# Transform along d of pairs 3 and 4 in two parts by lo, side by side in halves of the array's columns

## The chip, the cores and the metric

The kernel runs on one core of one Trainium2 chip. The metric is the device time of one execution in microseconds (us), the median of several runs. Profiles come from one more execution that the hardware profiler watched; its own time stands beside its span in the table below. Engines are named as the profile names them: PE (TensorE, the matrix multiplier), PEld (its weight loads), DVE (VectorE), ACT (ScalarE), POOL (GpSimd), SP (SyncE, which only issues DMAs here).

## The reference

Two kinds of layer alternate, twice each, on x of shape 1 x 2048 x 448 (S positions, D channels) in bf16:

```python
def _A_ref(x, w_r, w_i):
    X = rfft2(x.astype(float32), axes=(-2, -1))
    X = X * (w_r + 1j * w_i)
    return irfft2(X, s=(S, D), axes=(-2, -1)).astype(bfloat16)

def _B_ref(x, w1, b1, w2, b2):
    h = x @ w1 + b1
    h = relu(h) ** 2
    return h @ w2 + b2

x = x + _A_ref(layernorm(x), A_w_r, A_w_i)
x = x + _B_ref(layernorm(x), B_w1, B_b1, B_w2, B_b2)   # and both once more
```

`_A_ref` is a filter in the frequency domain: a Fourier transform over both axes, a product with complex weights, and the transform back. `_B_ref` is a feed-forward block with a squared relu and F = 1792.

## The kernel before, in words

**The spectral layer as matmuls.** A position s is split as s = 128 hi + lo, with hi from 0 to 15 and lo from 0 to 127. The layer goes through these stages, whose names are also the names of code:

- A: for each of 16 tiles of positions, a transform over hi together with the layer norm (`first_A`, `second_A`). Its result goes to `XA`, with d on the partitions and 16 components c of 128 values lo each. A tile t holds the eight values lo from 8t to 8t+7, so the first half of lo (0 to 63) is complete when tiles 0 to 7 are evicted, the second half with tile 15. The components are the real and imaginary parts (e = 0 and 1) of "pairs": pair p from 1 to 7 is components 2p and 2p+1; components 0 and 1 are the two real ones.
- TD: the transform along d (`stage_TD`), with a 128-column slice of `XA` as weights and the table `TD_sb` streaming. Its result, lo on the partitions, is evicted from PSUM to `U` in SBUF (`TD_out`).
- B: the transform over lo (`stage_B`), from `U` through the tables `G_sb` and `GN_sb` into `EF`.
- W: the product with the complex weights on DVE (`stage_W`), from `EF` into `Z`: first pair 1 alone, then pairs 2 and 3, then 4 and 5, then 6 and 7, then components 0 and 1.
- Bi, TI, AI: the transforms back; AI's result is added to x on DVE (L1147).

The feed-forward layer then computes h (`h_part`, `h_pairs`) and the output tiles o (`o_tile`), PE's large part of the work. In the first feed-forward layer each output tile is followed by the second spectral layer's stage A for that tile (`second_A`), so that the second TD follows the last tiles of the first feed-forward layer. Dummy matmuls (L1416, `warm_mm`) are put in where the planner sees PE idle for long.

**Pairs 1 and 2 in halves.** `TD_half` (L912) computes one e of pairs 1 and 2 together. It has two parts h = 0 and 1, one for each half of lo, and each is a unit of its own: the weights are 64 columns of `XA`, the matmuls of pair 1 and pair 2 alternate, and they go to different halves of the array's columns, and so to different halves of the PSUM partitions (s in L920). Part 0 needs only stage A's tiles 0 to 7. For the second pair of the two the halves of lo come out exchanged, and row L106 exchanges the rows of its table `G` to match. Each of the two pairs has a PSUM bank for itself and a 448-column eviction. Pair 4 (it is in `SPLIT`) has a bank and a 448-column eviction for each e, with full 128-column weights; pair 3 has two banks and one 896-column eviction for both e.

**What sets the order.** Each matmul group, eviction or vector operation is a unit, numbered in the order in which the code makes it. The strings in `ORDER` (L115) list for each engine the units in the order in which that engine issues them; an engine runs its list strictly in that order, and semaphores make it wait for what a unit needs. PSUM has eight banks, which are given out along the list of PE. The units that matter here, by their numbers before the change:

- First layer: 156 is the last of stage A on PE, 157 and 160 evict its last tiles. TD of pairs 1 and 2: 161 and 162 (e = 0, part 0 and 1), evicted by 163 (pair 1) and 164 (pair 2); 165 and 166 (e = 1), evicted by 167 and 168. B of pair 1: 169 and 171, evicted by 170 and 172. W of pair 1: 173 to 180. B of pair 2: 181 and 183. TD of pair 3: 185. B of pair 3: 187 and 189. TD of pair 4: 199 and 201. TD of pair 5: 207.
- Second layer: 857 is stage A of the last tile on PE, evicted by 858 (pairs 0 to 3) and 859 (pairs 4 to 7). TD of pairs 1 and 2: 860 and 861, 864 and 865, evicted by 862, 863, 866, 867. B of pair 1: 868 and 870, evicted by 869 and 871; of pair 2: 880 and 878, evicted by 881 and 879. W of pair 1: 872 to 877. TD of pair 3: 882. B of pair 3: 884, evicted by 885. TD of pair 4: 894 and 896.

Of the kernel before, what the change touches and what calls it, by code (L numbers as in the profile page):

```python
# [25 lines left out]
MERGE = (1, 2, 3, 4, 5)  # L26

# [9 lines left out]
def make_constants():  # L37
# [68 lines left out]
    G[:, 3] = np.roll(G[:, 3], 64, axis=0)  # L106
# [20 lines left out]
1354""",  # L127
    "act": """
# [12 lines left out]
1310 1313 1315 1318 1320 1323 1325 1330 1328 1335 1333 1338 1340""",  # L141
    "dve": """
# [438 lines left out]
def bass_interleave_layers__spectral_gfnet__dense_activation_squared_relu__prompt_kernel(nc, A_x, A_w_r, A_w_i, B_x, B_w1, B_b1, B_w2, B_b2, out):  # L581
# [6 lines left out]
    with ExitStack() as es:  # L588
# [220 lines left out]
        q = _Tile(1)  # L809
# [102 lines left out]
        def TD_half(first, e):  # L912
# [26 lines left out]
            for i in range(2):  # L939
                TD_out(q[i], 2 * (1 + i) + e, 1, first, ("act", "dve"))  # L940
# [554 lines left out]
```

## Time and profile before

| What | Value |
|---|---|
| Time, median of 3 runs | 266.68 us (266.57 to 267.13) |
| The profiled execution | 267.61 us, its span 265.0 us |
| PE busy | 255.3 us (96%), 2127 matmuls |
| DVE busy | 203.7 us (77%) |
| ACT busy | 175.8 us (66%) |
| POOL busy | 14.2 us (5%) |
| Granted PE clock | 1.00 (mean) |

The time of the profiled execution is larger than the span by what lies before the first and after the last instruction (2.6 us). Rows of the timeline begin with the start in us from the span's start and the length; equal neighbours are put together with their count, and idle time of the engine before them stands in brackets with what ended it. A row of windows gives a stretch, its length, and the busy time of each engine in it with the number of instructions.

### The profile page before, as it was taken

How to read it: one execution, taken by the hardware profiler on the slowest of the kernel's cores; microseconds unless marked ns; L12 is line 12 of the kernel's file. 1: busy time of each engine (PE TensorE's matmuls, PEld its weight loads, DVE VectorE, ACT ScalarE, POOL GpSimd, SP SyncE). 2: the span in 40 equal slices, each digit the busy share in tenths (PEclk: the TensorE clock that was granted, in tenths of full speed). 3: DMA queues.
4: the chain of work that ended last, by engine and by line, in shares of the span. 5: the costliest groups of instructions: out<-in, count | busy, mean ns of one | idle time of the engine just before them, and what ended most of it. 6: DMA issues, size and time to landing. Idle time of an engine off the chain costs nothing. (4 is left out here: it accounts for less than half of the span.)

```text
span 265.0 us, 5678 instructions
## 1 busy us (share of the span) xinstructions
PE 255.3 (96%) x2127; PEld 160.4 (61%) x2127; DVE 203.7 (77%) x653; ACT 175.8 (66%) x380; POOL 14.2 (5%) x32
## 2 busy tenths in 40 slices
PE   6999989999999999999999998899999999999996
PEld 2786678787544554455567775788654475554454
DVE  3988998999978973779996999899974239832552
ACT  5987898987549448793326988899645886311830
POOL 8840000000000000000000000000000000000000
PEclk9999999999999999999999999999999999999999
DMA  7999700023300223000000000020341000033022
GB/s 224 388 279 342 254 0 2 0 42 71 74 2 0 43 40 66 17 0 2 0 1 2 2 0 2 0 41 5 64 92 37 5 0 2 0 89 97 18 76 82
DMA packets 25531, 16.33 MB, mean 62 GB/s; under 512 B 18174, under 2 KB 24542, under 8 KB 25504
## 3 DMA queue, kind: packets, MB, share of 16 engines
q1 hardware_dynamic: 24768, 14.25, 20.4%
q10 hardware_dynamic: 576, 0.92, 1.0%
q0 software_dynamic: 160, 0.81, 0.7%
q8 instruction: 17, 0.28, 0.4%
q14 instruction: 10, 0.08, 0.1%
HBM read 10.46 MB, written 1.84 MB: 46 GB/s over the span
## 5 line engine op out<-in xcount | busy, mean ns | idle before, releaser
L681 PE MATMUL ps<-yT,W_sb 64*128 64x512 bf16 (+1 forms) x770 | 90.4, 346 | 0.0
L681 PE MATMUL ps<-W_sb,arena 128*128 128x448 bf16 (+3 forms) x476 | 87.1, 342 | 0.0
L681 PEld LDWEIGHTS ps<-yT,W_sb 64*128 64x128 bf16 (+1 forms) x770 | 52.6, 95 | 34.2 <-ACT arena L700 1.3
L735 DVE TENSOR_TENSOR arena<-arena 128x512 bf16<-128x512 bf16 (+1 forms) x140 | 44.8, 366 | 31.0 <-ACT arena L700 30.6
L681 PEld LDWEIGHTS ps<-W_sb,arena 128*128 128x128 bf16 x476 | 45.3, 98 | 38.3 <-DVE arena L735 1.5
L700 ACT ACTIVATE arena<-ps,b1col 128x512 bf16<-128x512 f32 x84 | 52.2, 688 | 24.5 <-PE ps L681 24.4
L706 ACT ACTIVATE arena<-ps 128x448 bf16<-128x448 f32 (+1 forms) x40 | 26.0, 717 | 5.5 <-PE ps L681 5.2
L700 ACT ACTIVATE mv<-mv,epst 128x1 f32<-128x1 f32 (+1 forms) x45 | 12.8, 294 | 14.7 <-DVE mv L826 13.4
L1171 ACT ACTIVATE VT<-x_sb 128x448 bf16<-128x448 bf16 x29 | 16.8, 582 | 5.5 <-DVE x_sb L1147 5.5
L700 ACT ACTIVATE arena<-ps 128x256 bf16<-128x256 f32 x56 | 17.9, 397 | 1.4 <-PE ps L681 1.1
L717 ACT ACTIVATE arena<-x_sb,rstd 128x448 bf16<-128x448 bf16 x13 | 8.8, 673 | 14.9 <-DVE rstd L1216 10.4
L706 ACT ACTIVATE XA<-ps 128x512 bf16<-128x512 f32 (+1 forms) x27 | 14.3, 581 | 4.3 <-PE ps L681 4.3
L681 PE MATMUL ps<-H_sb,arena 128*128 128x256 bf16 x128 | 15.9, 273 | 1.3 <-DVE arena L735 0.9
L681 PE MATMUL ps<-arena,G_sb 128*128 128x448 bf16 (+1 forms) x84 | 16.4, 335 | 0.2 <-ACT arena L706 0.2
L681 PE MATMUL ps<-yT,VT 64*128 64x512 bf16 x42 | 15.8, 376 | 0.0
L706 ACT ACTIVATE VT<-ps 128x1024 bf16<-128x1024 f32 (+2 forms) x20 | 14.1, 786 | 2.2 <-PE ps L681 2.1
L735 DVE TENSOR_TENSOR tmp<-arena,Wt 128x896 bf16<-128x896 bf16 x26 | 15.4, 622 | 0.1
L1293 DVE SCALAR_TENSOR_TENSOR x_sb<-ps,mv,arena 128x448 bf16<-128x448 f32 (+2 forms) x13 | 8.3, 645 | 9.3 <-PE ps L681 9.2
L681 PEld LDWEIGHTS ps<-H_sb,arena 128*128 128x128 bf16 x128 | 11.9, 98 | 4.9 <-DVE arena L735 2.9
L681 PE MATMUL ps<-TD_sb,XA 112*128 112x112 bf16 (+3 forms) x232 | 14.3, 230 | 0.3 <-DVE arena L707 0.3
L706 ACT ACTIVATE tmp<-ps 128x896 bf16<-128x896 f32 (+1 forms) x16 | 12.9, 849 | 1.5 <-PE ps L681 1.5
L681 PEld LDWEIGHTS ps<-TD_sb,XA 112*128 112x128 bf16 (+3 forms) x232 | 12.3, 103 | 2.2 <-DVE arena L707 0.5
(84 smaller groups left out, 298.5 us busy)
## 6 DMA issues: line engine op xcount, KB each, us to landing
out_dram<-x_sb SPq DMA_DIRECT2D x15, 112.0 KB, 1.8
W_sb<-in_B_w_dram SPq DMA_DIRECT2D x1, 1568.0 KB, 12.4
W_sb<-in_B_w_dram SPq DMA_DIRECT2D x1, 1344.0 KB
xin<-in_A_x_dram ACTq DMA_DIRECT2D x4, 224.0 KB, 5.5
xin<-in_A_x_dram SPq DMA_DIRECT2D x4, 224.0 KB, 7.0
H_sb<-c_H SPq DMA_DIRECT2D x1, 896.0 KB, 7.0
G_sb<-c_G SPq DMA_DIRECT2D x1, 672.0 KB, 9.5
Wt<-in_A_w_i_dram SPq DMA_DIRECT2D x1, 393.8 KB, 5.6
```

The source lines that it names most:

```text
L681: return sch.add("pe", lambda e: e.matmul(_res(o), lhsT, rhs, start=start, stop=stop, skip_group_check=skip), [lhsT, rhs], [o], cost=cost, ...
L700: sch.add("act", lambda e: e.activation(o, _res(i), func, **kw), rd, [o], cost=c)
L706: op = sch.add(engs[0], lambda e: e.activation(o, _res(i), ACT.Copy) if h[0].eng == "act" else e.tensor_copy(o, _res(i)), [i], [o], cost=c ...
L717: op = sch.add(engs[0], lambda e: e.activation(o, i, ACT.Copy, scale=s) if h[0].eng == "act" else e.tensor_scalar(o, i, s, 1.0, op0=ALU.mu ...
L735: sch.add(eng, lambda e: e.tensor_tensor(o, _res(a), b, op), [a, b], [o], cost=_free(o) / rate + 69.0)
L1171: op = sch.add("act", lambda e, i=i, o=o, x=x, h=h: e.activation(o, x, ACT.Square, accum_out=sd[:, i, 1:2]) if h[0].eng == "act" else e.sc ...
L1293: small(lambda e: e.scalar_tensor_tensor(out=o, in0=_res(i), scalar=rs[0] if rs else 1.0, in1=xi, op0=ALU.add if t >= 4 and last else ALU. ...
```

## The change

Pairs 3 and 4 get the same treatment as pairs 1 and 2: for each e, two parts by the halves of lo, with the two pairs side by side in the halves of the array's columns. `TD_half` takes the two pairs as an argument; the rows of `G` are exchanged for pair 4, too, as they are for pair 2. Pair 3 no longer has one 896-column eviction but two of 448 columns. There are two units more in each of the two spectral layers, so that later units are renumbered, and the planner's lists of all five engines are new throughout.

```diff
+COUPLES = ((1, 2), (3, 4))
...
-    G[:, 3] = np.roll(G[:, 3], 64, axis=0)
+    for _, p in COUPLES:
+        G[:, p + 1] = np.roll(G[:, p + 1], 64, axis=0)
...
-        def TD_half(first, e):
+        def TD_half(first, e, pair):
...
-                    p, s = 1 + i, slice(64 * (h ^ i), 64 * (h ^ i) + 64)
+                    p, s = pair[i], slice(64 * (h ^ i), 64 * (h ^ i) + 64)
...
-                TD_out(q[i], 2 * (1 + i) + e, 1, first, ("act", "dve"))
+                TD_out(q[i], 2 * pair[i] + e, 1, first, ("act", "dve"))
...
-            if p == 2:
-                return
-            if p == 1:
-                for e in range(2):
-                    TD_half(first, e)
-                return
+            for pair in COUPLES:
+                if p == pair[0]:
+                    for e in range(2):
+                        TD_half(first, e, pair)
+                if p in pair:
+                    return
```

The lists of PE, the lines around the two transforms along d:

```diff
-54 70 62 104 78 107 86 94 117 120 143 146 130 133 159 156 161 165 162 166 185 171 169 207 181 187 183 189 199 201 211
-205 209 203 225 221 227 223 251 247 239 249 255 241 253 259 261 263 257 265 267 287 374 289 270 392 291 318 272 304
...
-843 822 807 837 727 860 757 857 864 861 865 882 868 870 880 878 884 902 894 896 914 904 900 898 918 938 930 920 916
...
+70 54 62 78 104 107 86 120 117 94 146 143 130 133 159 156 161 185 165 189 162 166 190 186 171 169 181 183 195 209 193
+205 213 207 227 223 211 229 225 253 241 249 251 257 243 255 265 263 259 261 267 269 289 376 272 291 394 274 293 320
...
+809 845 744 729 824 862 839 888 759 859 866 863 867 884 889 870 872 885 882 880 892 906 904 922 902 908 918 924 920
```

In the new numbers the first layer keeps 0 to 184. Pairs 3 and 4 are 185 and 186 (e = 0, part 0 and 1, evicted by 187 and 188) and 189 and 190 (e = 1, evicted by 191 and 192); B of pair 3 is 193 and 195, and units from B of pair 4 on have 2 more than before. In the second layer the units up to B of pair 2 have 2 more than before; pairs 3 and 4 are 884 and 885 (e = 0) and 888 and 889 (e = 1), evicted by 886, 887, 890 and 891; B of pair 3 is 892, and units from B of pair 4 on have 4 more.

In the new lists of the evicting engines, the first TD's evictions stand as 163, 164, 187 and then 172 on DVE, and 167, 168, 188, 170, 192, 191 on ACT (before: 163, 168, 172 on DVE and 167, 164, 170, 186 on ACT). In the second layer the old 859 goes from DVE, where it came just ahead of W of pair 1, to ACT, right behind 858; ACT then has 864, 869 (the old 862 and 867), 890, 891, 873 (the old 871), 886, 887, 883, 881, 893.

In stage A of the first layer, where x still arrives by DMA, DVE's list before has 84 (the reciprocal for tile 4, from which POOL's 85 scales the table for PE's 86) and 110 ahead of 135, the first statistics of tile 12; the new one has them behind it.

More of the change, by code (lines that the diff above doesn't have):

```diff
@@ L116 @@
     "pe": """
[10 rows of a table removed]
-1354""",
-    "act": """
[12 rows of a table removed]
-1310 1313 1315 1318 1320 1323 1325 1330 1328 1335 1333 1338 1340""",
-    "dve": """
[23 rows of a table removed]
-1339 1341 1346 1255 1343 1119 1349 1352 1355""",
[10 rows of a table added]
+1355 1358""",
+    "act": """
[12 rows of a table added]
+1117 1312 1317 1319 1314 1324 1322 1327 1329 1334 1332 1339 1337 1342 1344""",
+    "dve": """
[23 rows of a table added]
+1262 1340 1338 1343 1345 1353 1350 1347 1356 1359""",
     "pool": """
-12 15 13 16 17 14 18 20 19 22 21 53 69 61 23 77 24 85 25 116 119 26 142 145 129 132 158 155""",
+12 15 13 16 18 17 20 14 19 22 21 69 53 61 77 23 25 85 119 116 24 145 142 129 132 26 155""",
     "sp": """
-3 6 4 8 10 28 30 29 36 32 40 41 39 31 27 34 45 37 33 47 46 38 44 35 314 334 269 352 354 355 372 390 408 426 1005 1026
-1044 1046 1064 1047 1082 1100 1306 1303 1118 1297 1300 1206 1203 1250 1347 1259 1256 1212 1253 1350 1209 1344 1353
-1356""",
+3 6 4 8 10 30 28 29 38 45 36 32 35 40 34 41 31 33 46 44 27 39 47 37 316 336 354 271 356 357 374 392 410 428 1009 1030
+1048 1050 1068 1051 1086 1307 1310 1104 1301 1122 1210 1263 1216 1213 1207 1304 1260 1254 1354 1257 1351 1348 1357
+1360""",
 }
```

84 rows, old and new, of the table ORDER are left out of this document.

## The prediction

> **What bounds the kernel now.** First the page's busy times, then the windows, cut where the timeline shows the kernel's stages to change.
>
> ```profile
> PE 255.3 (96%) x2127; PEld 160.4 (61%) x2127; DVE 203.7 (77%) x653; ACT 175.8 (66%) x380; POOL 14.2 (5%) x32
> ```
> ```profile
> core 0: us, PE busy (x) PEld busy (x) DVE busy (x) ACT busy (x) POOL busy (x), PEclk, DMA share, GB/s
> 21.60:40.80 19.20, 18.28 (x139) 12.80 (x137) 18.96 (x39) 17.10 (x25) 0.00 (x0) 1.00 0.54 172
> 49.80:141.00 91.20, 91.20 (x708) 53.56 (x706) 78.54 (x303) 56.59 (x138) 0.00 (x0) 1.00 0.13 26
> 148.20:165.50 17.30, 16.13 (x163) 11.73 (x160) 17.10 (x34) 15.32 (x22) 0.00 (x0) 1.00 0.01 2
> 173.00:262.70 89.70, 89.69 (x678) 52.04 (x676) 55.47 (x158) 50.65 (x117) 0.00 (x0) 1.00 0.18 43
> ```
>
> The page alone says PE, at 96%. The windows say where that is true: in the two feed-forward layers (91.20 of 91.20 us and 89.69 of 89.70) PE has no idle time, and a start that is x us later there is passed on as x us. In the spectral layers it is DVE: 18.96 of 19.20 us and 17.10 of 17.30, from the first operation of stage W to its last, at 21.60 to 40.80 and at 148.20 to 165.50. PE idles in both. So a spectral layer ends as late as W starts, plus 19 or 17 us of DVE work that the change leaves as it is. The question is what the change does to the first W operation (pair 1's). The timelines of the three engines ahead of it, first layer (PE, DVE, ACT):
>
> ```profile
> 17.05 0.27 PE L681 MATMUL ps<-Fs,m 128*128 128x256 bf16 x1
> 17.25 1.76 PE L681 MATMUL ps<-TD_sb,XA 128*64 128x224 bf16 x32
> 19.32 0.94 PE L681 MATMUL ps<-TD_sb,XA 128*128 128x224 bf16 x8 [0.31 <-DVE arena L707]
> 20.09 0.92 PE L681 MATMUL ps<-arena,G_sb 128*128 128x448 bf16 x4
> ```
> ```profile
> 18.63 1.16 DVE L707 CAST arena<-ps 128x448 bf16<-128x448 f32 x2 [0.94 <-PE ps L681]
> 20.67 0.62 DVE L707 CAST arena<-ps 128x448 bf16<-128x448 f32 x1 [0.88 <-PE ps L681]
> 21.63 0.69 DVE L735 TENSOR_TENSOR tmp<-arena 128x448 bf16<-128x448 bf16 x2 [0.33 <-ACT arena L706]
> ...
> 24.24 0.62 DVE L735 TENSOR_TENSOR tmp<-arena,Wt 128x896 bf16<-128x896 bf16 x1
> ```
> ```profile
> 15.85 2.10 ACT L706 ACTIVATE XA<-ps 128x512 bf16<-128x512 f32 x4
> 19.02 0.98 ACT L706 ACTIVATE arena<-ps 128x448 bf16<-128x448 f32 x2 [1.06 <-PE ps L681]
> 21.05 3.68 ACT L706 ACTIVATE arena<-ps 128x448 bf16<-128x448 f32 x6 [1.06 <-PE ps L681]
> ```
>
> PE does the halves of pairs 1 and 2 (32 matmuls), waits for a bank, does pair 3 (x8), then B of pair 1 (x4, at 20.09). Its evictions end on ACT at about 21.6, and W starts at 21.63. DVE and ACT sit idle in between: the path is matmul, eviction, matmul, eviction.
>
> **The matmuls themselves cost the same.** Matmuls overlap, so I use the distance of their starts: length less one matmul, over one less than the count. The 32 halves take (1.76 - 0.26) / 31 = 0.048 us each, the 8 whole ones (0.94 - 0.26) / 7 = 0.097. Two halves for one whole: 0.39 us for a unit of 8 halves, and four units (1.56) for the three units that go (0.78 and twice 0.39). Loads double in number, of 64 columns each:
>
> ```profile
> L681 PEld LDWEIGHTS ps<-TD_sb,XA 128*128 128x128 bf16 x48 | 4.5, 98 | 1.1 <-DVE arena L707 0.5
> L681 PEld LDWEIGHTS ps<-TD_sb,XA 128*64 128x64 bf16 x32 | 1.5, 109 | 0.3 <-DVE XA L707 0.2
> L706 ACT ACTIVATE arena<-ps 128x896 bf16<-128x896 f32 x18 | 15.8, 921 | 1.4 <-PE ps L681 1.4
> L706 ACT ACTIVATE arena<-ps 128x448 bf16<-128x448 f32 x22 | 11.2, 550 | 4.1 <-PE ps L681 3.9
> ```
>
> A load of half the columns takes 109 ns instead of 98. It hides behind the other half's matmul, or the halves could not follow each other every 48 ns. (TensorEngine Tiling (Array Packing) of the Trainium skill, under Restrictions and Gotchas, says that column tiling excludes the fast weight load. The two load rows agree; with loads that were not hidden, the 32 halves would need 3.5 us and not 1.76, so the rule does not bind here.) Eviction: one of 921 and two of 550 ns become four of 550, or 620 on DVE (20.67), 0.2 to 0.3 us more in each layer, some of it on a DVE that waits anyway.
>
> **First layer: W starts 0.4 us later.** The new list of PE is 161 185 165 189, 162 166 190 186, 171 169: all first parts, then all second parts, then B of pair 1. From 17.25, eight units of 0.39 end at 20.38. Entering the split mode costs 0.20 - 0.11 = 0.09 us (17.05 to 17.25 against the normal distance of stage A); I take the same for leaving it: B can start at 20.47, where it started at 20.09. Its input is ready by then: pair 1's second part is done after six units, at 19.6; ACT starts an eviction about 0.2 after the matmuls (18.8 to 19.02) and takes 0.55, so 20.35. From B to W the path keeps its length, 21.63 - 20.09 = 1.54, since ACT's 188 is done by 21.3 and B's first result waits for ACT until 21.4: W at 22.0, **0.4 us later**. The gap that the change fills (18.8 to 19.32) lay ahead of B, but two units of second parts (0.78) came ahead of pair 1's, and two behind them; what leaves the place is one pair-3 unit of 0.78 and the wait. Bounds: 0, if B were not held up; 0.8, if pair 3's last eviction (ACT's 191, sixth in a row from 19.8, about 22.8) also holds up B of pair 3 and opens a gap in W of pairs 2 and 3. DVE gets there 24.24 - 21.63 = 2.61 after W's start, at 24.6 (24.24 is that operation's start before). Its input: B of pair 1 and the two units of pair 2 (0.19 a matmul, 0.76 a unit of four) end at 22.75, pair 3's unit waits for 191 and ends at 23.6, its eviction at 24.4. So no gap: 0.4.
>
> **Second layer: 0.1 us.** PE, DVE, ACT:
>
> ```profile
> 141.02 1.06 PE L681 MATMUL ps<-Fs,tmp 128*128 128x128 bf16 x16
> 142.01 0.58 PE L681 MATMUL ps<-TD_sb,XA 112*64 112x112 bf16 x16
> 142.82 0.40 PE L681 MATMUL ps<-Fs,tmp 128*128 128x128 bf16 x4 [0.23 <-DVE mv L744]
> 143.06 0.38 PE L1416 MATMUL ps<-ones 128*128 128x512 bf16 x1
> 143.72 0.39 PE L681 MATMUL ps<-Fs,tmp 128*128 128x64 bf16 x8 [0.29 <-DVE Fs L718]
> 144.04 0.58 PE L681 MATMUL ps<-TD_sb,XA 112*64 112x112 bf16 x16
> 144.56 0.34 PE L1416 MATMUL ps<-ones 128*128 128x256 bf16 x2
> 144.83 1.87 PE L681 MATMUL ps<-TD_sb,XA 112*64 112x112 bf16 x48
> 146.57 2.43 PE L681 MATMUL ps<-arena,G_sb 128*128 128x448 bf16 x12
> ```
> ```profile
> 145.84 1.93 DVE L707 CAST arena<-ps 128x448 bf16<-128x448 f32 x3 [2.27 <-PE ps L681]
> 147.69 0.41 DVE L707 CAST XA<-ps 128x256 bf16<-128x256 f32 x1
> 148.19 1.17 DVE L735 TENSOR_TENSOR tmp<-arena,Wt 128x896 bf16<-128x896 bf16 x2
> 149.46 0.69 DVE L735 TENSOR_TENSOR tmp<-tmp 128x448 bf16<-128x448 bf16 x2
> ```
> ```profile
> 142.63 1.91 ACT L706 ACTIVATE XA<-ps 128x512 bf16<-128x512 f32 x4
> 145.45 0.98 ACT L706 ACTIVATE arena<-ps 128x448 bf16<-128x448 f32 x2 [0.91 <-PE ps L681]
> 146.74 4.46 ACT L706 ACTIVATE arena<-ps 128x896 bf16<-128x896 f32 x7 [0.31 <-PE ps L681]
> ```
>
> Here idle PE time really lies ahead of B: PE waits for DVE's last tile (142.4 to 143.72) and then for its eviction (to 144.83). But only one first part (888) is put there; pairs 1 and 2's second parts still start at about 144.83, when ACT has evicted the tile (144.54) and two dummy matmuls are through, and B of pair 1 at 146.54, when DVE's second eviction of its input is in (146.47): before, pair 3 stood between them, now two units of halves, and both fit. ACT, behind two new evictions of 0.44 net from 146.63, reaches B's second result at 147.5; before, it had pair 3's one of 0.92 there from 146.74. W starts at 148.15. Then 885 stands ahead of B of pairs 2 and 3: 0.39 and two changes of mode at 0.09, 0.57 us. ACT then has five evictions of 0.44 from 147.5 and one of 0.92, and so the input of W of pairs 2 and 3 at 150.6 to 150.75; DVE arrives there, after two operations (148.19 to 149.46 before) and four of 0.30, at 150.6. Bounds: 0 and 0.57; I take **0.1**. The eviction at 147.69 that moves from DVE to ACT fits in ACT's idle time before 145.45. (The same page says under Tiling Modes that a change of mode drains the array: the 0.09 agrees. The new list has 18 changes for 14; by the rule all four more would cost PE 0.4 us, but two lie in its idle time.)
>
> **What else moves.** All lists are new. Where PE is at 91.20 of 91.20, another order can win nothing and may lose something. In stage A, 84 stands behind 135, which waits for x:
>
> ```profile
> 10.42 1.16 DVE L825 BATCH_NORM_STATS2 st<-xin 128x6 f32<-128x448 bf16 x2 [0.61 <-DMA xin<-in_A_x_dram]
> 12.23 0.28 PE L681 MATMUL ps<-Fs,xin 128*128 128x256 bf16 x1 [0.17 <-ACT Fs L717]
> ```
>
> PE stalls 0.33 there before (11.90 to 12.23); with tile 4's table made after 11.2 it stalls earlier instead and as long or 0.1 longer. Bounds -0.3 (the stall goes) to 0.5; I take **0.1**. The stretches between W and the feed-forward layers (40.80 to 49.80 and 165.50 to 173.00) keep their operations in nearly the same order: 0, within 0.3 either way.
>
> **The sum**: 0.4 + 0.1 + 0.1 = 0.6 us on a span of 265.0 and a profiled execution of 267.61, so 265.6 and 268.2. The median of the runs is 0.93 below the profiled execution; carried over, 266.68 + 0.6 = **267.3 us**.
>
> **The rivals.**
> - *PE is what is short* (faster). If the start of W did not count, PE's filled idle time would: 0.5 us at 18.8 and 0.39 for 888, so 0.9 less, 265.8. It decides where DVE has slack in W; 18.96 of 19.20 speaks against it. Chance 0.17.
> - *Nothing is passed on* (no change). B of pair 1 is late, but the new order makes it good in stage A or between W and h: 266.7. For it speaks the 0.33 stall in stage A. Chance 0.2.
> - *A new stall behind the halves* (slower). Eight halves hold all eight PSUM banks, and ACT has six evictions in a row; if it falls behind, B of pairs 2 and 3 opens gaps in W in both layers, 0.4 each, besides the 0.6: 268.1. It decides when the W operations of pairs 2 and 3 are reached before B's evictions; I have margins of only 0.2 and about -0.1. Chance 0.2.
> - My forecast, W later by 0.5 in all, from 266.9 to 267.8: chance 0.43.
>
> **How the numbers follow.** A measurement of this kernel can tell about 0.2%, 0.53 us, from no change. Faster has 0.17. Same: the 0.2 and a third of the forecast's 0.43 (what lies below 267.2), 0.35. Slower: the rest, 0.48. The range goes from 265.8, the first rival's own time, to 268.4, the third rival's with the 0.3 of the unknown stretches: outside lie half of the first and a quarter of the others' tails, about 2 in 10. Without the faster rival it would be 266.6 to 268.4.
>
> **What would show it.** In the changed kernel's timeline: 64 halves in one run of about 3.3 us from 17.3, B of pair 1 at about 20.5, W's first operation at 22.0 to 22.2 and then DVE without a gap over 0.2; in the second layer B to W as before relative to the last tile, and a gap of about 0.1 before W of pairs 2 and 3; PE without idle time in the feed-forward layers. The prediction is wrong if W starts at or before 21.6, if stage A ends more than 0.4 from 17.2, or if PE shows new waits in the feed-forward layers.

## The result, and the profile after

The changed kernel takes 267.16 us (median of 17 runs, 266.88 to 267.79), the kernel before 266.66 us beside it (17 runs, 266.44 to 267.29). The ratio is 1.0017, 95% interval 1.0009 to 1.0024: 0.45 us slower, with 0.24 to 0.64. The forecast was 267.3, 0.6 slower. The profiled execution of the changed kernel took 266.91 us, its span 265.1.

The busy line of its page (as before: time, share, instructions), then the windows from the first W operation to the end of the layer's DVE work and from the first to the last matmul of each feed-forward layer:

```profile
PE 257.8 (97%) x2178; PEld 166.2 (63%) x2178; DVE 203.1 (77%) x655; ACT 175.3 (66%) x381; POOL 13.6 (5%) x31
```
```profile
21.66:40.71 19.05, 18.58 (x139) 12.88 (x137) 18.88 (x38) 15.89 (x24) 0.00 (x0) 1.00 0.49 164
49.74:140.96 91.22, 91.22 (x708) 55.77 (x706) 77.61 (x302) 57.39 (x139) 0.00 (x0) 1.00 0.13 26
148.01:165.45 17.44, 15.76 (x149) 11.15 (x147) 17.20 (x34) 15.95 (x23) 0.00 (x0) 1.00 0.01 1
172.93:262.79 89.86, 89.86 (x678) 54.94 (x676) 55.88 (x161) 49.24 (x114) 0.00 (x0) 1.00 0.18 43
```

The picture is the same as before: DVE without a pause in W, PE without one in the feed-forward layers. PE's 1% more on the page is no sign of less waiting; part of it is dummy matmuls, six of them in one row (1.47 us) while PE waits for W in the first layer. The timeline around the change, PE, DVE and ACT:

```profile
16.50 0.27 PE L683 MATMUL ps<-Fs,m 128*128 128x256 bf16 x1
16.70 3.26 PE L683 MATMUL ps<-TD_sb,XA 128*64 128x224 bf16 x64
19.89 1.50 PE L683 MATMUL ps<-arena,G_sb 128*128 128x448 bf16 x7
...
36.89 1.47 PE L1418 MATMUL ps<-ones 128*128 128x512 bf16 x6
```
```profile
18.84 2.31 DVE L709 CAST arena<-ps 128x448 bf16<-128x448 f32 x4 [1.79 <-PE ps L683]
21.66 0.69 DVE L737 TENSOR_TENSOR tmp<-arena 128x448 bf16<-128x448 bf16 x2 [0.51 <-ACT arena L708]
```
```profile
19.23 1.42 ACT L708 ACTIVATE arena<-ps 128x448 bf16<-128x448 f32 x3 [1.50 <-PE ps L683]
20.86 1.42 ACT L708 ACTIVATE arena<-ps 128x448 bf16<-128x448 f32 x3 [0.21 <-PE ps L683]
```

All 64 halves run in one row of 3.26 us, and B of pair 1 starts 3.19 us after the first of them (before: 20.09 - 17.25 = 2.84). The first W operation comes 4.96 us after the first half (before 21.63 - 17.25 = 4.38). Its absolute time hardly moved, 21.66 for 21.63, because the first half itself started 0.55 earlier.

Since the start of stage A differs from run to run, I measure all kernels from the first half. In this table S is the start of the first half, B that of B of pair 1, W that of the first W operation, h that of the first matmul of the feed-forward layer; "W length" goes to the start of W's last operation; "FF2" is from the first to the last matmul of the second feed-forward layer. FF2 goes to the end of its last matmul; all others are differences of starts in the timelines. The ratio is to the kernel before, measured beside each (medians 266.60 for e1 to e4, 266.63 for e5 to e8, 266.69 for e9 to e12).

| Kernel | Time, us | Ratio, 95% interval | S to B | B to W | W length | S to h | FF2 |
|---|---|---|---|---|---|---|---|
| before | 266.66 | | 2.84 | 1.54 | 18.79 | 32.55 | 89.72 |
| after | 267.16 | 1.0017 (1.0009 to 1.0024) | 3.19 | 1.77 | 18.66 | 33.04 | 89.86 |
| e1 before, new stage A | 267.49 | 1.0038 (1.0025 to 1.0052) | 3.39 | 1.53 | 18.78 | 33.09 | 89.72 |
| e2 after, old stage A | 267.33 | 1.0030 (1.0019 to 1.0041) | 3.19 | 1.77 | 18.66 | 33.04 | 89.85 |
| e3 before, 4 matmuls ahead of B | 268.39 | 1.0069 (1.0055 to 1.0083) | 2.84 | 2.30 | 18.78 | 33.30 | 90.65 |
| e4 after, other order | 267.66 | 1.0037 (1.0025 to 1.0048) | 2.94 | 1.54 | 19.18 | 33.29 | 89.86 |
| e5 before, 7 matmuls in Bi | 268.35 | 1.0064 (1.0050 to 1.0078) | 2.84 | 1.54 | 18.78 | 33.26 | 90.65 |
| e6 before, 2 matmuls ahead of B | 268.21 | 1.0053 (1.0040 to 1.0066) | 2.85 | 1.91 | 18.77 | 32.92 | 90.64 |
| e7 after, order found later | 267.37 | 1.0022 (1.0012 to 1.0031) | 2.53 | 1.95 | 19.10 | 33.00 | 89.85 |
| e8 before, B of pair 1 earlier | 266.77 | 1.0009 (0.9998 to 1.0021) | 2.15 | 1.96 | 18.95 | 32.45 | 89.95 |
| e9 before, 4 matmuls at the start | 267.90 | 1.0042 (1.0029 to 1.0055) | 2.84 | 1.54 | 18.79 | 32.55 | 90.60 |
| e10 e8, eviction back on ACT | 266.60 | 0.9997 (0.9988 to 1.0006) | 2.15 | 1.57 | 19.26 | 32.36 | 89.72 |
| e11 e7 with three changes | 266.75 | 0.9999 (0.9990 to 1.0008) | 2.53 | 1.56 | 19.02 | 32.53 | 89.71 |
| e12 e2, one eviction to ACT | 267.66 | 1.0039 (1.0026 to 1.0052) | 3.19 | 1.54 | 19.02 | 33.17 | 89.86 |

Read the first two lines: 0.49 us in the first layer (+0.35 to B, +0.23 from B to W, -0.13 in W, the rest behind it), and 0.14 in the second feed-forward layer. Between them, from h to the first matmul of the second feed-forward layer, it is 123.17 before (172.97 - 49.80) and 123.19 after. In the second spectral layer small terms cancel: PE and DVE of the changed kernel,

```profile
141.72 0.58 PE L683 MATMUL ps<-TD_sb,XA 112*64 112x112 bf16 x16
...
144.13 2.32 PE L683 MATMUL ps<-TD_sb,XA 112*64 112x112 bf16 x80
146.39 0.93 PE L683 MATMUL ps<-arena,G_sb 128*128 128x448 bf16 x4
147.25 0.58 PE L683 MATMUL ps<-TD_sb,XA 112*64 112x112 bf16 x16
```
```profile
148.01 1.17 DVE L737 TENSOR_TENSOR tmp<-arena,Wt 128x896 bf16<-128x896 bf16 x2 [0.41 <-ACT arena L708]
149.28 0.69 DVE L737 TENSOR_TENSOR tmp<-tmp 128x448 bf16<-128x448 bf16 x2
150.08 0.69 DVE L737 TENSOR_TENSOR arena<-tmp 128x448 bf16<-128x448 bf16 x2
150.69 1.16 DVE L737 TENSOR_TENSOR tmp<-arena,Wt 128x896 bf16<-128x896 bf16 x2
```

The first half (141.72) comes 91.98 us after h, 0.23 sooner than before (142.01 - 49.80 = 92.21); B of pair 1 comes 4.67 behind it (before 146.57 - 142.01 = 4.56), and the row of DVE from the first W operation to its end is 17.44 us long (before 165.50 - 148.19 = 17.31). W of pairs 2 and 3 (150.69) follows without a wait for B. The gap of 0.1 us stands ahead of 150.08, where an operation reads what the one right before it wrote, and not where I looked for it.

### The profile page after: what moved, and what is told of

It reads as the page before. It is cut to its first block, busy times and chain, and to the rows that moved or that the text cites. A ratio compares the mean times of both kernels' runs of the same rounds, so it can differ in the third digit from the quotient of the medians.

```text
span 265.1 us, 5774 instructions
## 1 busy us (share of the span) xinstructions
PE 257.8 (97%) x2178; PEld 166.2 (63%) x2178; DVE 203.1 (77%) x655; ACT 175.3 (66%) x381; POOL 13.6 (5%) x31
## 4 chain that ended last, share of the span: by engine, by line
PE 81%; DVE 13%; issue 3%; DMA 1%; ACT 1%; DVEq 0%
PE ps L683 81%; DVE tmp L737 8%; DVE arena L737 3%; DMA xin<-in_A_x_dram 1%; ACT arena L708 1%; PE ps L1418 1%; DVE VT L709 1%; DVE x_sb L1149 0%; DVE st L827 0%; DVE VT L1174 0%; DVE VT L737 0%; DVE x_sb L1295 0%; DVE mv L828 0%; DVE x_sb L741 0%; DVEq L1431 0%
## 5 line engine op out<-in xcount | busy, mean ns | idle before, releaser
L683 PEld LDWEIGHTS ps<-yT,W_sb 64*128 64x128 bf16 (+1 forms) x770 | 56.6, 95 | 29.0 <-ACT arena L702 2.0
L708 ACT ACTIVATE arena<-ps 128x448 bf16<-128x448 f32 (+1 forms) x41 | 25.3, 698 | 5.2 <-PE ps L683 5.0
L683 PE MATMUL ps<-TD_sb,XA 112*64 112x112 bf16 (+3 forms) x280 | 14.3, 229 | 0.0
L683 PEld LDWEIGHTS ps<-TD_sb,XA 112*64 112x64 bf16 (+3 forms) x280 | 12.7, 106 | 2.2 <-issue 0.8
L683 PEld LDWEIGHTS ps<-arena,G_sb 128*128 128x128 bf16 x84 | 7.6, 98 | 5.7 <-ACT arena L708 1.2
```

The lines of the kernel that those rows point to most:

```text
L683: return sch.add("pe", lambda e: e.matmul(_res(o), lhsT, rhs, start=start, stop=stop, skip_group_check=skip), [lhsT, rhs], [o], cost=cost, ...
L708: op = sch.add(engs[0], lambda e: e.activation(o, _res(i), ACT.Copy) if h[0].eng == "act" else e.tensor_copy(o, _res(i)), [i], [o], cost=c ...
```

## The experiments

My theory: what stands ahead of B of pair 1 delays W, and DVE, which bounds the layer, passes it on one for one. Rivals: PE's idle time takes such a delay up; and the new order of stage A, or the halves as such, make the difference.

**e1 and e2: stage A.** The two kernels with each other's lists up to the first half. The lists of PE:

```diff
 e1, the kernel before:
-54 70 62 104 78 107 86 94 117 120 143 146 130 133 159 156 161 165 162 166 185 171 169
+70 54 62 78 104 107 86 120 117 94 146 143 130 133 159 156 161 165 162 166 185 171 169
 e2, the changed kernel:
-70 54 62 78 104 107 86 120 117 94 146 143 130 133 159 156 161 185 165 189 162 166 190 186 171 169
+54 70 62 104 78 107 86 94 117 120 143 146 130 133 159 156 161 185 165 189 162 166 190 186 171 169
```

> The kernel before, with the order of stage A (every list up to the first transform along d, and the loads of x) taken from the changed kernel; pairs 3 and 4 stay whole. In the two profiles the first transform along d starts at 16.70 us in the changed kernel and at 17.25 before. Theory (the 0.55 us is the arrival of x, which differs from run to run, and not the order): the time is that of before within 0.2 us, and the start of the first transform lies anywhere from 16.7 to 17.3. Rival (the new order of stage A is worth 0.5 us, and the halves cost 1 us): 0.4 to 0.6 us below before, 266.1 to 266.3.

> The changed kernel with stage A in the order of before. Theory (the order of stage A is worth nothing, the halves and what follows them cost the 0.5 us): 267.1 to 267.3, as the changed kernel. Rival (the new order gives 0.5 us and hides half of what the halves cost): 0.4 to 0.6 above the changed kernel, 267.6 to 267.8. A third: the changed kernel loses its 0.5 us in stage A; then this one is as fast as before, 266.7.

e1 is 0.7 to 1.4 us slower than before, which neither theory had. Its timeline of PE shows half a microsecond of it; beside it, e2, the kernel with the halves and the old stage A, with PE, DVE and the feed-forward layer's start:

```profile
16.82 0.96 PE L681 MATMUL ps<-TD_sb,XA 128*64 128x224 bf16 x16
18.17 0.96 PE L681 MATMUL ps<-TD_sb,XA 128*64 128x224 bf16 x16 [0.39 <-ACT XA L706]
```
```profile
16.90 3.26 PE L683 MATMUL ps<-TD_sb,XA 128*64 128x224 bf16 x64
...
21.86 0.69 DVE L737 TENSOR_TENSOR tmp<-arena 128x448 bf16<-128x448 bf16 x2 [0.51 <-ACT arena L708]
...
49.94 1.26 PE L683 MATMUL ps<-yT,W_sb 128*128 128x256 bf16 x10
```

In e1 the second parts of pairs 1 and 2 wait for ACT's last eviction of stage A (18.17; without it they would follow at 17.6). The changed kernel has the first parts of pairs 3 and 4 in that place. So the new stage A and the new halves belong together, and the halves do fill a wait, one that only the new stage A opens. The remaining 0.35 us of e1's median lies in no stretch behind the first half (h to the second feed-forward layer 123.10, FF2 89.72); the place left is stage A with its variation, which this one profile, of an execution of 266.94, does not show.

e2 is the clean comparison, with stage A as before: every column of its line is that of the changed kernel to 0.01, and its time is 0.5 to 1.1 us above before. The trace gives 0.49 in S to h, 0.00 from there to the second feed-forward layer (173.11 - 49.94 = 123.17) and 0.13 in FF2: 0.62. Whether the new stage A gains what lies between e2 and the changed kernel (0.2 by the medians, 0.35 by the ratios) is not shown: the intervals overlap.

**e3, e6: more work ahead of B.** The first matmul of B of pair 1 is issued four times more (e6: twice):

```diff
                     q = _Tile(1)
+                    if first and p == 1 and e == 1:
+                        for _ in range(4):
+                            mm(q[lambda b: ps[:, b, 0:2 * LW]], G_sb[:, i, a, :], ur, True, True, skip=True)
                     mm(q[lambda b: ps[:, b, 0:2 * LW]], G_sb[:, i, a, :], ur, True, False)
```

> The kernel before, whose first matmul of B of pair 1 in the first layer is issued four times more ahead of the one that counts (its result is overwritten, so the output is the same): 4 x 0.19 = 0.76 us of PE work right ahead of the path to W, which PE can make good later, since it idles 0.9 us in W. Theory (DVE bounds the spectral layer, and what delays the start of W delays the end): W starts 0.7 later and the time grows by 0.6 to 0.8 us, to 267.3 to 267.5. Rival (PE is short, and idle PE time takes the delay): 0 to 0.2 us.

> Half the earlier dose: two extra matmuls (0.38 us) ahead of B of pair 1 instead of four. Four gave 1.7 to 1.8 us: 0.75 at the start of W, passed on to the end of the first spectral layer unchanged, and 0.93 in the second feed-forward layer, where one DMA transpose landed late beside a fetch of instructions. Theory (the start of W is passed on one for one, and the rest was that one collision): 0.3 to 0.45 us above before, 266.9 to 267.05. Rival (every delay of the layer costs more than itself): 0.8 to 0.9. If the collision comes at this dose too, 1.2 to 1.4, with one gap of about 0.9 in the second feed-forward layer in the profile.

0.76 us of matmuls make S to h 0.75 longer, 0.38 make it 0.37 longer. W's length stays at 18.78, and the idle time of PE takes up nothing. So far the theory holds to a hundredth. But both kernels lost 0.92 to 0.93 us more, in FF2. The view of DMA packets from 185 to 191 us (a digit is the busy share of 0.15 us in tenths), before and e3, and the landing of the transposes that are issued from 183 to 194 us:

```profile
DMA  0000000000000499999997000000500000000000
...
DMA to landing us min/median/max: 3.0/3.1/3.1
```
```profile
DMA  0000000000000002999999993300000000000000
...
DMA to landing us min/median/max: 3.1/3.9/4.7
```

Nine slices of a DMA transpose, then a lone 5: a fetch of instructions, 16 KB on queue q8, at 189.3 us, 16.4 after that layer's start at 172.97. In e3 it comes at 188.8, 15.5 after the start at 173.32, right on the transpose's end, and the transpose lands 4.7 us after its issue instead of 3.1. ACT and PE of e3 a moment later:

```profile
190.93 0.67 ACT L717 ACTIVATE arena<-x_sb,rstd 128x448 bf16<-128x448 bf16 x1 [2.29 <-DMA yT<-arena]
...
194.27 3.01 PE L681 MATMUL ps<-W_sb,arena 128*128 128x448 bf16 x15 [0.76 <-DVE arena L735]
```

The write over the transposed buffer waits 2.29 us, and PE, which bounds this layer, then 0.76. (The Trainium skill, Advanced Engine Details and Errata, ISA Cache, gives 16 KB, 256 instructions, as the unit in which instructions are cached; the trace's fetches on q8 are of that size.)

**e9: the same instructions where they do nothing.** Four narrow matmuls among the dummies at the start:

```diff
+                if ename == "pe" and k == 4:
+                    for _ in range(4):
+                        sch.narrow[op](eng)
                 ins = op.fn(eng)
```

> The kernel before with four small matmuls more (128 columns, about 0.1 us each, results never used) among the dummy matmuls at the very start, where PE waits for x: no work on any path. The three kernels before with 2, 4 and 7 extra matmuls all show one more loss, of 0.93 us, in the second feed-forward layer, where a fetch of 16 KB of instructions at 15.46 us after that layer's start (16.38 without the extra matmuls) meets a DMA transpose. Theory (the extra instructions move the fetch, whatever they do themselves): the fetch comes at about 15.5, the transpose lands 4.7 instead of 2.9 us after its issue, PE stands still for 0.9, and the time is 0.8 to 1.0 above before, 267.4 to 267.7. Rival (the delay of the first spectral layer shifts the two against each other): no loss, 266.5 to 266.8.

S to h is 32.55 as before, and FF2 is 90.60: the loss comes without any delay of the layer. ACT, PE and the landings of e9:

```profile
190.13 0.67 ACT L719 ACTIVATE arena<-x_sb,rstd 128x448 bf16<-128x448 bf16 x1 [2.25 <-DMA yT<-arena]
...
193.46 3.77 PE L683 MATMUL ps<-W_sb,arena 128*128 128x448 bf16 x19 [0.71 <-DVE arena L737]
```
```profile
DMA to landing us min/median/max: 3.1/3.9/4.6
```

So the extra instructions move the fetch, and the rival is out. The time rose by 0.8 to 1.5 us; the trace accounts for 0.88. The other profiles bear out the link: in all fourteen together, none of the 149 transposes without a fetch on q8 between issue and landing took more than 3.3 us, and of the 15 with one, eleven took 4.4 to 4.9 and four 3.1 to 3.3. The changed kernel, with other lists, meets no fetch at this place. It meets one at an earlier transpose, issued at 103.2 us and landed 4.4 us later, and S to h and the first feed-forward layer show nothing of it.

**e5: a control in the wrong place.**

```diff
                     k = lb if m else 0
+                    if first and p == 6 and lb == 0:
+                        for _ in range(7):
+                            mm(q[lambda b: ps[:, b, 0:256]], G_sb[:, 7, 0, :], H_sb[:, 7, 0, :], True, True, skip=True)
```

> Control to the four extra matmuls ahead of B: the kernel before with seven extra matmuls (0.76 us, results overwritten) later in the first layer, at the start of a Bi unit of pair 6, where PE idles 0.7 us behind stage W. Theory (DVE bounds the layer, PE has slack there): 0 to 0.2 us. Rival (PE work counts wherever it stands): 0.7 to 0.8 us.

The extra work cost 0.71 us in S to h, besides the 0.93 of the fetch. It stood behind PE's wait and not in it: the end of W releases a row of Bi matmuls that leads straight on to TI, and a matmul there is on the path. The control thus says nothing for or against PE's slack. The changed kernel is the better one: its 1.47 us of dummies at 36.89 stand ahead of that wait, and from W's last operation to h it is 9.42 us there (28.08 - 18.66) for 9.38 before (28.17 - 18.79).

**e4, e7: another order of the halves.** The lists of PE from the first half on:

```diff
-161 185 165 189 162 166 190 186 171 169 181 183 195 209 193 205
+161 165 162 166 185 189 171 169 190 186 181 183 195 193 209 205
 e7 (with the stage A of before):
+189 161 165 162 166 185 171 169 190 186 183 195 181 193 209 207
```

> The changed kernel with the halves in another order in the first layer: both parts of pairs 1 and 2, then the first parts of pairs 3 and 4, then B of pair 1, and the second parts of pairs 3 and 4 behind it; the evictions are listed to match. Two units of 0.39 us and two changes of mode leave the path to the first W operation. Theory (what stands ahead of B of pair 1 is paid in full): W starts 0.4 to 0.8 us earlier after the first half than in the changed kernel, and the time is 0.3 to 0.6 us below it, 266.6 to 266.9. Rival (the evictions of pairs 3 and 4 come late instead and open gaps in W of pairs 2 and 3): W starts earlier, gaps of 0.3 to 0.8 us appear behind it, and the time is the changed kernel's or up to 0.5 above.

> The changed kernel with stage A in the order of before, and in the first layer another order of the same units: one half-unit of pairs 3 and 4 ahead of everything, then both parts of pairs 1 and 2, one more half-unit of pairs 3 and 4, B of pair 1, and the last two half-units behind it; the evictions and the W operations are listed to match, so that a W operation seldom stands right behind the one that it reads from. Theory (the halves cost nothing as such; what stands ahead of B of pair 1 and the order of DVE's list does): W starts 0.3 to 0.5 us earlier after the first half than in the changed kernel, W is no longer, and the time is 266.7 to 267.0. Rival (the halves cost in themselves, by changes of mode and twice as many evictions): 267.2 to 267.4, as the changed kernel.

W starts 0.48 (e4) and 0.48 (e7) earlier after S, as foreseen, and nothing of it arrives at h: W is 0.52 and 0.44 longer. No wait for PE stands in it, and for ACT only one in e4 that loses 0.07 (at 25.30). DVE's operations otherwise overlap by 0.08 us; these lists put some right behind the operation that they read from, and there a gap of 0.03 or 0.10 stands instead, 0.12 or 0.19 lost at each place (the gap ahead of 150.08 above is one). e4's stage A shows besides a wait for POOL's table of tile 4 that the changed kernel's own profile, with the same lists there, does not have:

```profile
11.89 0.27 PE L683 MATMUL ps<-Fs,xin 128*128 128x256 bf16 x1 [0.47 <-POOL Fs L720]
```

**e12: the 0.23 us between B and W.** In e2 one eviction moves, 187, from DVE ahead of W's inputs to ACT behind 170:

```diff
-DVE 163 164 187 172 174     ACT 167 168 188 170 192 191
+DVE 163 164 172 174         ACT 167 168 188 170 192 187 191
```

> The changed kernel with stage A in the order of before, and one eviction (first half-unit of pair 3) moved from DVE to ACT, behind the eviction of B of pair 1, so that DVE idles 0.1 to 0.2 us ahead of its last eviction in front of W. Theory (the 0.23 us that W starts later behind B is DVE's own, and goes when DVE idles before that eviction): from B to W 1.54 to 1.6 us instead of 1.77. Rival (it comes from ACT or from elsewhere): 1.77. For the time, either: ACT is later by 0.44 us for the inputs of pairs 2 and 3, 267.1 to 267.8.

DVE of e7, where the evictions ahead of W run without a pause, and of e12:

```profile
18.77 2.22 DVE L709 CAST arena<-ps 128x448 bf16<-128x448 f32 x4 [1.33 <-PE ps L683]
21.49 0.69 DVE L737 TENSOR_TENSOR tmp<-arena 128x448 bf16<-128x448 bf16 x2 [0.51 <-ACT arena L708]
```
```profile
20.52 0.62 DVE L709 CAST arena<-ps 128x448 bf16<-128x448 f32 x1 [0.48 <-PE ps L683]
21.47 0.69 DVE L737 TENSOR_TENSOR tmp<-arena 128x448 bf16<-128x448 bf16 x2 [0.33 <-ACT arena L708]
```

B to W is 1.54 again. In e12, and in the nine other kernels whose rows show 0.33, W begins 0.03 us behind the end of ACT's eviction of B of pair 1, so the releaser that the rows name fits there. In the changed kernel that eviction (20.86, 0.54 long) had ended 0.26 us before W began, in e2 also 0.26, in e7 and e8 0.42: there ACT is not what holds W, and what does is not shown. Nor is it shown whether the pause counts or the number of evictions: these four kernels have four DVE evictions in one unbroken row ahead of W, the other ten have three and a pause ahead of the last. But ACT's extra eviction now comes ahead of the inputs of pairs 2 and 3, W is 0.36 longer, and S to h is worse than in e2.

**e8, e10: the kernel before with B of pair 1 first.**

```diff
-PE 161 165 162 166 185 171 169 207     DVE 163 168 172         ACT 167 164 170 186
+PE 161 165 162 166 171 169 185 207     DVE 163 168 164 172     ACT 167 170 186       (e8)
+PE 161 165 162 166 171 169 185 207     DVE 163 168 172         ACT 167 164 170 186   (e10)
```

Both also exchange neighbours in DVE's list of W: before 176 175 177 178 191 180 193 179, in e10 175 176 178 177 180 193 179 191. e8 has further exchanges in the second layer.

> The kernel before, pairs 3 and 4 whole, with B of pair 1 ahead of the first unit of pair 3 in the first layer, and a few neighbours exchanged in both layers. Theory (W starts as early as B of pair 1 lets it): 0.1 to 0.3 us below before, 266.3 to 266.5. Rival (the evictions of pair 3 then come late for W of pairs 2 and 3): the time of before or up to 0.3 above.

> The kernel before with B of pair 1 ahead of the first unit of pair 3 in the first layer, as in the earlier kernel of this kind, but with the second layer and the order of the feed-forward layers as before, and with the eviction that had been given to DVE back on ACT, so that DVE idles ahead of its last eviction in front of W. In all kernels so far W starts 0.33 us behind that eviction where DVE idled ahead of it, and 0.51 where it did not. Theory: W starts 0.2 to 0.3 us earlier after the first half than in that earlier kernel, the second feed-forward layer takes 89.72 us again, and the time is 0.3 to 0.5 us below before, 266.1 to 266.3. Rival (W's later operations wait for their inputs or for one another, and the end of the layer stays): 266.5 to 266.8.

e10 has W 0.66 us earlier than before after S, and W is 0.47 longer; S to h gains 0.19, and the time shows no difference (0.9988 to 1.0006). The rival is right: what is won at the start is mostly lost inside W. Eight of W's operations start behind a gap there, and four before. Two of the eight, at 23.64 and 25.16 (the second of the row at 24.49), wait for ACT's evictions of the inputs of pairs 2 and 3 and lose 0.28 us together; the others stand right behind the operation that they read from. DVE and ACT of e10:

```profile
23.18 0.39 DVE L735 TENSOR_TENSOR arena<-tmp 128x448 bf16<-128x448 bf16 x1
23.64 0.63 DVE L735 TENSOR_TENSOR tmp<-arena,Wt 128x896 bf16<-128x896 bf16 x1
```
```profile
20.72 2.82 ACT L706 ACTIVATE arena<-ps 128x896 bf16<-128x896 f32 x4 [0.22 <-PE ps L681]
```

The window of e10's W against that of before (same 38 instructions):

```profile
20.53:39.79 19.26, 18.55 (x144) 13.35 (x142) 18.94 (x38) 16.73 (x24) 0.00 (x0) 1.00 0.58 189
```
```profile
21.63:40.42 18.79, 17.87 (x136) 12.50 (x134) 18.58 (x38) 16.69 (x24) 0.00 (x0) 1.00 0.55 175
```

DVE's busy share is 98% and 99%. e8's FF2 is longer by 0.23 us, which was not followed up; e10, with the later lists as before, does not have that. A window that is full does not say that it is short.

**e11: the halves without their cost.** e7 with 164 on ACT, the first W operations as in the changed kernel, and the lists of the second feed-forward layer as before:

```diff
-DVE 163 168 164 172 173 174 176 175 178 177 198 200 179 180     ACT 167 170 191 187
+DVE 163 168 172 174 173 175 176 178 177 198 179 200 180         ACT 167 164 170 191 187
```

> The changed kernel with the other order of the first layer (both parts of pairs 1 and 2 first, B of pair 1 ahead of the last two half-units), and three changes beside: an eviction in front of W from DVE to ACT, so that DVE idles ahead of the last one; the first W operations in the order of the changed kernel; and the second feed-forward layer in the order of before. Theory: W starts 0.2 to 0.3 us earlier than in the first kernel with that order, W is 0.1 shorter, the second feed-forward layer takes 89.72 us again instead of 89.85; 266.8 to 267.0, between before and the changed kernel. Rival (what is won at the start of W is lost to W operations that wait): 267.2 to 267.4.

```profile
17.27 2.49 PE L683 MATMUL ps<-TD_sb,XA 128*64 128x224 bf16 x48
...
49.80 1.37 PE L683 MATMUL ps<-yT,W_sb 128*128 128x256 bf16 x11
```
```profile
172.99:262.70 89.71, 89.71 (x678) 52.04 (x676) 55.48 (x158) 50.63 (x117) 0.00 (x0) 1.00 0.18 43
```

S to h is 32.53 (before 32.55), FF2 89.71 (89.72), the time that of before: 266.75, ratio 0.9990 to 1.0008, and below all the other kernels with the four pairs in halves. So a kernel with the halves can be as fast as before, and what the changed kernel loses comes with its order: the units ahead of B, the evictions on DVE ahead of W, and one order of the second feed-forward layer. That the halves cost nothing in an equally good order is not shown: e10, with whole pairs, has S to h 0.17 shorter than e11 (32.36), though the two times cannot be told apart. None of the versions beats the kernel before beyond the interval.

## Why the prediction was right, point by point

- **What bounds the kernel**: right for a delay, and shown by e3 and e6: it is passed on one for one, and PE's idle time takes up none of it. The rival "PE is what is short" is out. For a gain it does not hold as written: W's length was taken as fixed, and in e4, e7 and e10, where W starts earlier, it is 0.44 to 0.52 us longer.
- **The cost of the halves**: right. 64 halves in 3.26 us are (3.26 - 0.26) / 63 = 0.048 each, and e11 has them at no loss of time. The reason given was wrong: a half's load does not hide behind the other half's matmul. In the trace the matmuls of two halves start 3 to 4 ns apart, and so do their loads; the next pair of matmuls follows after 0.096 us, less than the 0.110 of a load, so the loads hide behind the pair ahead. The 3.5 us for loads that do not hide counted them one by one. The 18 changes of mode for 14 do not come out either: the traces have 10 steps into or out of the 64-column form, and 8 before.
- **First layer, forecast 0.4, found 0.49.** B of pair 1 came 0.35 later for 0.38. The step "from B to W the path keeps its length" failed: it grew by 0.23, and with one eviction fewer on DVE ahead of W it does not (e12; why is open). W itself was 0.13 shorter, which I had not worked out: it has one gap fewer, three for four. That the sum of these comes within 0.1 of the forecast is luck.
- **Second layer, forecast 0.1, found 0.02** (e2: 0.00). The number is near by luck: B of pair 1 came 0.11 later behind the first half and the row of W was 0.13 longer, neither of them forecast, but PE reached the first half 0.23 sooner behind the feed-forward layer; the unit ahead of B of pairs 2 and 3 held up nothing.
- **Stage A, forecast +0.1**: the size is not settled. It ended 0.5 from the 17.2 of my sign, outside the 0.4 that I had set (16.70), so by that sign this part was wrong. The wait at tile 4 that I expected in the new order is not in the changed kernel's profile and is in e4's, with 0.47 us of idle time. Most of the 0.55 can be variation: in eleven profiles with the old stage A, before among them, the first half starts at 16.74 to 17.27, in three with the new one at 16.70, 16.82 and 17.48.
- **The stretches taken at 0**: right for those between W and h. But "another order can win nothing and may lose something" was said of the feed-forward layers and then entered as 0: the second one lost 0.14, with the same 678 matmuls and no wait in it. e11, with the order of before, has it back. This is the term that the sum put at nothing without a reason; what in the order costs the 0.14 was not followed up.
- **The sum**: 0.49 + 0.02 + 0.14 = 0.65 in the trace with equal stage A (forecast without stage A: 0.5); measured 0.45, 0.24 to 0.64, by a new stage A that may give 0.2 back. Misses of both signs lie in a forecast that is 0.14 us off; its mechanism held in the first layer, and the rest of the closeness is luck.
- **The rivals**: "a new stall behind the halves" did not come; W of pairs 2 and 3 had its inputs in time in both layers. "Nothing is passed on" is out as a mechanism. That stage A makes part good stays open.
- The sign "W's first operation at 22.0 to 22.2" failed by the clock (21.66) and held by distance (4.96 us behind S, forecast 4.75). I had tied the signs to absolute times, though one execution's stage A was in them.

## What to carry to other kernels

Measure an edit from the last event ahead of it, and not from the start of the span: here arrival and stage A move everything by up to half a microsecond. Where an engine is full, earlier inputs help only if its own list stays well mixed; an order that starts 0.5 us earlier and puts dependent operations side by side gives it all back. And a change of a few instructions can move a fetch of code onto a DMA far away: look for a second step in the trace before the whole difference is put down to the edit.

## What I had not expected of the hardware

- Two, four or seven matmuls more ahead of 188 us moved a 16 KB fetch from 16.4 to 15.4 or 15.5 us after the second feed-forward layer's start. There it made a transpose land in 4.6 to 4.7 us for 3.0 to 3.1 and cost 0.88 to 0.93 us, in four kernels of four (e3, e5, e6, e9). Why three different numbers move it by the same 0.9 is open, and so is which fetch does harm: 2.4 us behind the issue of a transpose, one goes with a landing of 4.7 (e7, at 105.8) and one with 3.2 (e8, at 187.5).
- Where four DVE evictions ran without a pause ahead of W (the changed kernel, e2, e7, e8), the first W operation started 0.51 us behind the last of them, although ACT's eviction of its other input had ended 0.26 to 0.42 before. Where there were three and a pause of 0.23 us or more (before, e1, e3 to e6, e9 to e12), it started 0.33 behind DVE's last and 0.03 behind ACT's. e12 and e10 switch it by moving one eviction. The cause was not found.
- A DVE operation that reads the result of the one right before it starts 0.12 to 0.19 us later than one that doesn't: 0.03 or 0.10 behind the reported end of the one ahead, and not 0.08 before it.
